# Block-sparse attention feeding a cosine router: x's writes on another queue, some copies and turns placed elsewhere

## The chip, the core and the metric

The kernel runs on one NeuronCore of one Trainium2 chip, in one launch. TensorE multiplies and transposes, VectorE (DVE), ScalarE (ACT) and GpSimd (POOL) work element by element, and transfers between DRAM and the on-chip memory are issued into queues by SyncE (SP), ScalarE or GpSimd and carried by 16 DMA engines. The metric is device time in microseconds, lower is better; a run gives one such time, and the median of several is quoted.

## The reference

Attention over 4 sequences, 8 heads, 768 positions and 64 numbers a head, in blocks of 32. A query block sees its neighbours, the first and the last block, and three blocks drawn for it; the first and last query block see all. The result goes, as 3072 rows x of 512 numbers, through a router that picks one of 8 experts by the cosine of x with an embedding, and through that expert:

```
scores = scale * q @ k.T;  scores = where(mask, scores, -1e9)
attn   = exp(scores - max) / (sum + 1e-9);   x = (attn @ v).transpose(0, 2, 1, 3).reshape(3072, 512)
logits = (x / |x|) @ (emb / |emb|).T / tau;  e = argmax(logits);  gate = softmax(logits)[e]
out    = gate * (relu(x @ w1[e]) @ w2[e])        # w1: 8 x 512 x 1024, w2: 8 x 1024 x 512
```

All of it is float32.

## The kernel before, in words

**Tiles.** A chunk is 128 queries of one sequence with all 8 heads; there are 24. Two chunks at the same place of two sequences are a duo (12 of them), and the loads, the routing and the rows of x go by duos. `pair_chunk` gives the place; place 0, which holds the first and last query block of a sequence, belongs to chunks 0, 1, 22 and 23, and these alone also do the "ends" (every key of the sequence).

**The attention loop** (`attention_fast`) has 25 steps s. In step s the scores of chunk `TURNS[s]` are made (`now`), the chunk of the step before is weighed with its values and normalized (`last`), the chunk of two steps before is transposed for the router (`past`, `turn_x`), and the next chunk's queries and keys are brought into shape (`after`). `TURNS` is 0, 2, 1, 3, 4, 5 and so on, so chunk 1 is scored in step 2. Nothing is reordered here: inside `manual_schedule` each engine and each queue does its work in the order of the code. Outside, in the expert tiles, a planner orders the instructions.

In one step TensorE does: `score_near` (L586, L589), `score_far` (L611), in even steps from 6 on `sum_logits` (L778), `turn_x` (L746), `turn_q` (L545), in steps 10 to 12 `turn_k` (L532), then weighs: `weigh_far`, the router's `part_logits` in odd steps (L768), `weigh_near` (all weighing is L666). ScalarE follows with the exponentials (L594, L616), the copies of own values `stack` in odd steps (L463), the copy of `part` (L770), the copy of the logits `take_logits` (L790) and the square of x (L736). VectorE has `gather_k` (L555), the copies after `turn_x` (L749) and `turn_q` (L550), the small operations of `route`, and `normalize` (L718, L720, L731). GpSimd copies the other gathered keys (L568) and values from neighbours (L511).

**Buffers that make work wait.** `turn_x` and `part_logits` share one PSUM buffer, `xg_ps`. The weighted sums `av` have one PSUM buffer, so `sum_logits` of a step, which opens it anew, waits until `normalize` of the step before has read it. The rows of x have three buffers, one per duo: `normalize` of duo s + 3 waits until duo s has been written to DRAM. The PSUM buffers "big" are two.

**Transfers.** In the loop every transfer but two query loads at the start is on SP's queue, in code order. Per step that is the gathering of 6 value blocks (`gather_v`, 128 KB each, address read from a register; L499), and between them loads of queries, keys and values (L497, L501). A gather for the next duo but one can be issued when `weigh_far` has read the buffer.

**The router** of a duo is a generator (`route`) whose six pieces `after_step` deals out over the steps that follow; the last piece writes x to DRAM (L887) and stands in the middle of a step (`planned(0)`): for duo 0 in step 7, for duo 1 in step 8, for duo b in step 2b + 6, up to duo 8 in step 22. Duo 0 has two pieces of rows, the others here one. Duos 9 and 10 are written behind the loop, when `k.attending` is false, and duo 11 during the first expert tile.

**The end of the loop.** Step 23 (chunk 22) and step 24 (chunk 23) are "ends" steps: `score_ends` for head pairs 0 and 2 (L642), `weigh_far`, `weigh_ends` for 0 and 2, `score_ends` for 1 and 3, `weigh_ends` for 1 and 3, `weigh_near`. The last step ends with the transposes of the first expert tile. Then 25 expert tiles follow, whose weights (2 MB each of w1 and w2) come on SP's queue.

The lines that the change touches most:

```
    copy = nc.scalar.copy if g % 2 or b == 0 else nc.vector.tensor_copy          # turn_k
    for half in range(1 if c == 0 else 0, 2):                                    # gather_k, near keys
        for z in range(2):
            lo = BLK * (NG * c + 2 * half - 2 + 3 * z)
            copy_by_one_port(k, t[:, :, 2 * half + z, lanes_of(NRAND, z)], kt[:, :, lo:lo + BLK])
    for rows, lo in pieces(c):                                                   # route, last piece
        nc.sync.dma_start(out=dram[lo:...], in_=x[rows]...)
```

Of the kernel before, what the change touches and what calls it, by code (L numbers as in the profile page):

```python
# [16 lines left out]
ALU = mybir.AluOpType  # L17
AX = mybir.AxisListType
# [3 lines left out]
B, H, S, D = 4, 8, 768, 64  # L22
BLK = 32
NB = S // BLK
NRAND = 3
NC = S // P
# [356 lines left out]
def lanes_of(slot, g):  # L383

    if slot < 2:
        return slice(BLK + slot, NRAND * BLK, 2)
    return slice(0, BLK) if (slot + g) % 2 == 0 else slice(NRAND * BLK, P)
# [126 lines left out]
def turn_k(k, g):  # L514

    nc = k.nc
    b, j = divmod(g, NPAIR)
    kt = k.kt[b % 2]
    raw = k.raw.pop(("k", g))
    copy = nc.scalar.copy if g % 2 or b == 0 else nc.vector.tensor_copy  # L520
    if b < DUO:
        ps = k.big.tile([P, 1024], F32, name="kps", tag="big")
        for r in range(NC):
            for h in range(2):
                lo = (h * NC + r) * D
                nc.tensor.matmul(ps[D * h:D * (h + 1), r * P:(r + 1) * P], lhsT=raw[:, lo:lo + D], rhs=k.ident,
                                 start=True, stop=True)
        copy(out=kt[:, j, 0:S].rearrange("p (t r) -> p t r", r=NC), in_=ps[:, 0:S].rearrange("p (r t) -> p t r", r=NC))  # L528
    else:
        ps = k.big.tile([P, 2, 512], F32, name="kps", tag="big")  # L530
        for c in range(NC):
            nc.tensor.transpose(ps[:, c // 3, c % 3 * P:(c % 3 + 1) * P], raw[:, c * P:(c + 1) * P], k.ident)  # L532
        copy(out=kt[:, j, 0:S].rearrange("p (w t) -> p w t", w=2), in_=ps[:, :, 0:3 * P])
    if j == NPAIR - 1:
        for i, block in enumerate((NB - 1, 0)):
            copy = nc.scalar.copy if i or b else nc.vector.tensor_copy
            copy(out=kt[:, :, S + i * BLK:S + (i + 1) * BLK], in_=kt[:, :, block * BLK:(block + 1) * BLK])  # L537
# [14 lines left out]

def copy_by_one_port(k, out, in_):

    k.nc.vector.tensor_reduce(out=out, in_=in_.unsqueeze(3), axis=AX.X, op=ALU.max)  # L555


def gather_k(k, n):

    nc = k.nc  # L560
    b, c, _ = place(n)
    kt = k.kt[b % 2]
    k.kg[n] = t = k.gp.tile([P, NPAIR, NG, P], F32, name="kg", tag="kg")
    for s in range(NRAND):
        engine, copy = ((mybir.EngineType.Pool, nc.gpsimd.tensor_copy) if s else
                        (mybir.EngineType.DVE, partial(copy_by_one_port, k)))
        for g, shift in zip(blocks_of(c), shifts(k, engine, s, c)):
            copy(out=t[:, :, g, lanes_of(s, g)], in_=kt[:, :, bass.ds(shift, BLK)])  # L568
    for half in range(1 if c == 0 else 0, 2):
        for z in range(2):  # L570
            lo = BLK * (NG * c + 2 * half - 2 + 3 * z)
            copy_by_one_port(k, t[:, :, 2 * half + z, lanes_of(NRAND, z)], kt[:, :, lo:lo + BLK])


def score_near(k, n):
# [72 lines left out]
def weigh_ends(k, n, pairs):  # L648

    _, c, i = place(n)  # L650
    for m in range(NC):
        for odd in range(2):
            for j in pairs:
                h = 2 * j + odd
                to = side(c, h, 0)
                weigh(k, n, slice(D * to, D * (to + 1)), h, k.pb[j][:, m, odd], k.vt[m][:, i, h])


def weigh(k, n, lanes, h, lhsT, rhs, last=False):

    av, begun = k.av[n]
    quads = [(h // NPAIR, q) for q in range(lanes.start // BLK, lanes.stop // BLK)]
    first = [q not in begun for q in quads]
    assert all(first) or not any(first)
    begun.update(quads)
    k.nc.tensor.matmul(av[lanes, h // NPAIR, h % NPAIR * P:h % NPAIR * P + D + 1], lhsT=lhsT, rhs=rhs, start=first[0],  # L666
                       stop=last, skip_group_check=True)
# [7 lines left out]
def weigh_near(k, n, turn):  # L675

    _, c, i = place(n)
    e, st = k.pac[n], k.st_ring[n // DUO % 2]
    for hh in range(2 * turn, 2 * turn + 2):
        for h in (hh, hh + NPAIR):  # L680
            for half in (1,) if c == 0 else (0, 1):
                to = side(c, h, half)
                weigh(k, n, slice(D * to, D * (to + 1)), h, e[:, h // 2, half, D * (h % 2):D * (h % 2 + 1)],
                      st[:, half, i, h], turn == 1)


def weigh_far(k, n, part):
# [147 lines left out]
def route(k, b):  # L835

    nc, p, x = k.nc, k.rp, k.x[b]
    many = NC if k.exact else DUO
    nrm = p.tile([P, many], F32, name="nrm") if k.exact else k.nsq[b]
    if k.exact:  # L840
        for c in range(NC):
            sq = p.tile([P, ND, P], F32, name="sq")
            nc.scalar.activation(sq, x[:, c, :, 0:P], ACT.Square, accum_out=nrm[:, c:c + 1])
    nc.gpsimd.tensor_tensor(out=nrm, in0=nrm, in1=k.half[:, 0:many], op=ALU.pow)

    def wide(t):
        return t.unsqueeze(2).broadcast_to([P, many, E])

    l = p.tile([P, many, E], F32, name="l")
    lg = logits(k, x) if k.exact else k.lg[b]  # L850
    yield
    nc.vector.tensor_scalar(out=nrm, in0=nrm, scalar1=1e-6, scalar2=None, op0=ALU.add)
    nc.vector.reciprocal(out=nrm, in_=nrm)
    m = p.tile([P, many], F32, name="mx")
    nc.vector.tensor_tensor(out=l, in0=lg, in1=wide(nrm), op=ALU.mult)
    nc.vector.reduce_max(out=m, in_=l, axis=AX.X)
    nc.vector.tensor_tensor(out=l, in0=l, in1=wide(m), op=ALU.subtract)
    yield
    ex = p.tile([P, many, E], F32, name="ex_l")
    nc.scalar.activation(ex, l, ACT.Exp)  # L860
    oh = k.oh[:, b * many:(b + 1) * many, :]
    pick = p.tile([P, many, E], F32, name="pick")
    nc.vector.tensor_scalar(out=pick, in0=l, scalar1=0.0, scalar2=None, op0=ALU.is_equal)
    nc.vector.tensor_tensor(out=pick, in0=pick, in1=k.rev.unsqueeze(1).broadcast_to([P, many, E]), op=ALU.mult)
    nc.vector.reduce_max(out=m, in_=pick, axis=AX.X)
    picked = nc.vector.tensor_tensor(out=oh, in0=pick, in1=wide(m), op=ALU.is_equal).ins
    yield
    for c in range(many):
        t = b * many + c
        nc.gpsimd.tensor_tensor(out=k.seen[:, t + 1, :], in0=k.seen[:, t, :], in1=k.oh[:, t, :], op=ALU.add)  # L870
    for w in (4, 2):
        nc.gpsimd.tensor_tensor(out=ex[:, :, 0:w], in0=ex[:, :, 0:w], in1=ex[:, :, w:2 * w], op=ALU.add)
    gate = p.tile([P, many, 1], F32, name="gate")
    nc.gpsimd.tensor_tensor(out=gate, in0=ex[:, :, 0:1], in1=ex[:, :, 1:2], op=ALU.add)
    nc.gpsimd.tensor_scalar(out=gate, in0=gate, scalar1=1e-9, scalar2=None, op0=ALU.add)
    yield
    with ExitStack() if k.attending else k.tc.issue_after(picked):
        nc.vector.reciprocal(out=x[:, :, :, P], in_=gate.broadcast_to([P, many, ND]))
    yield
    if k.exact:  # L880
        nc.sync.dma_start(out=k.x_dram[b * S:(b + 1) * S, :].rearrange("(c p) w -> p c w", p=P),
                          in_=x.rearrange("p c e w -> p c (e w)"))
        return
    a, c = pair_chunk(b)
    dram = k.x_dram[DUO * S * a:DUO * S * (a + 1), :].rearrange("(i s) w -> s i w", i=DUO)
    for rows, lo in pieces(c):
        nc.sync.dma_start(out=dram[lo:lo + rows.stop - rows.start], in_=x[rows].rearrange("p i e w -> p i (e w)"))  # L887


def rank(k, b):  # L890
# [424 lines left out]
def attention_fast(n, ctx):  # L1315
# [77 lines left out]
    for s in range(NCH + 1):  # L1393
# [25 lines left out]
        if not late_keys:  # L1419
            keys_gathered()  # L1420
        summed, n.parted = n.parted, None
        if summed is not None:
            sum_logits(n, last)
        if past is not None and past >= 2 * DUO:
            turn_x(n, past)
        elif past is not None and past % DUO:
            turn_x(n, past - 1)
        if ends:
            score_ends(n, last, 0)
            score_ends(n, last, 2)  # L1430
        elif after is not None and s:
            turn_q(n, after)
        if past is not None and past < 2 * DUO and past % DUO:
            turn_x(n, past)
        if not ends:
            turn_keys()
        planned(0)
# [53 lines left out]
        for m in values_at.get(s, ()):  # L1491
            loads += load_v(n, 1, m)
        fetch_all(n, gathers, loads)
        if ends:
            weigh_ends(n, last, (1, 3))
        if last is not None:
            weigh_near(n, last, 0)
            weigh_near(n, last, 1)
            normalize(n, last, summed)
        if s == 0:  # L1500
            build_consts(n)
            next(experts)
# [232 lines left out]
```

## Time and profile before

| | us |
|---|---|
| median of 3 runs | 613.65 (611.6 to 614.97) |
| the profiled execution | 615.24 |
| its span, first to last instruction | 613.5 |
| TensorE busy | 587.9 (96%) |
| GpSimd, VectorE, ScalarE busy | 243.5, 238.7, 146.2 |
| the chain that ended last: TensorE, VectorE, DMA, SP's queue | 73%, 7%, 7%, 6% |
| granted TensorE clock, mean | 0.993 |

The span has two parts. Up to 245.91 us, where the first expert matmul starts, the attention loop runs, with all engines at work; from there TensorE runs through the expert tiles with next to nothing between them. A busy share is an average over both. In the rows below, "L666" is a line of the code, `av<-vg,pd` is the tile written and the tiles read, and `[0.35 <-DVE xt L749]` says that the engine idled 0.35 us ahead of this instruction until VectorE's instruction of L749 was done. The loop's steps are cut at the first matmul of `score_near`: steps 4 to 9 start at 58.32, 67.08, 76.31, 83.51, 90.70 and 103.02 us, step 11 at 119.64, step 13 at 140.62, step 23 at 218.00.

### The profile page before, as it was taken

Reading aid. Unit: us, or ns where it says so; the run is one execution under the profiler, and the core shown is the slowest. Engines: PE = TensorE matmul, PEld = TensorE weight load, DVE = VectorE, ACT = ScalarE, POOL = GpSimd, SP = SyncE. Lnnn points to the kernel's source line nnn. Section 1 sums busy time; section 2 is a strip of 40 time slices with the busy share of each in tenths; the row PEclk is TensorE's granted clock in tenths of the full one; section 3 lists DMA queues with packets and bytes.
Section 4 is the critical chain, followed back from the end, with each engine's and each line's share of the span. In section 5 each row is a group of like instructions: output and inputs, shape, how many; then the busy total and the mean of one; then the engine's idle time right before and its main releaser. Section 6 shows DMA issues by size and latency. Waiting matters only on the chain.

```text
span 613.5 us, 18777 instructions
## 1 busy us (share of the span) xinstructions
PE 587.9 (96%) x7736; PEld 454.2 (74%) x7736; DVE 238.7 (39%) x744; ACT 146.2 (24%) x286; POOL 243.5 (40%) x474
## 2 busy tenths in 40 slices
PE   8999997989999988999999999999999999999995
PEld 5898797878898877777777777746777736777772
DVE  4463584667779942476211211112221121121110
ACT  3535663566555552100000000000000000000000
POOL 2637636447765430320333333333333333333332
PEclk9999998999999998999999999999999999999999
DMA  8989789789988731999999999998999998999511
GB/s 204 242 172 207 165 173 214 167 199 202 208 204 198 208 120 38 336 397 398 407 392 400 408 366 338 341 332 303 408 402 392 401 380 311 391 403 404 224 36 35
DMA packets 177073, 170.60 MB, mean 278 GB/s; under 512 B 135432, under 2 KB 137608, under 8 KB 174162
## 3 DMA queue, kind: packets, MB, share of 16 engines
q1 hardware_dynamic: 170706, 155.61, 78.8%
q0 software_dynamic: 5216, 13.43, 6.0%
q8 instruction: 63, 1.03, 0.7%
q10 hardware_dynamic: 1056, 0.26, 0.2%
q14 instruction: 32, 0.26, 0.1%
HBM read 156.65 MB, written 12.90 MB: 276 GB/s over the span
## 4 chain that ended last, share of the span: by engine, by line
PE 73%; DVE 7%; DMA 7%; SPq 6%; issue 3%; POOL 2%; ACT 1%; POOLq 0%; DVEq 0%; ACTq 0%
PE hp L1224 26%; PE yp L1237 25%; PE av L666 6%; SPq L499 4%; PE dps L611 4%; DMA vg<-in_v_dram 2%; PE hp L1269 2%; PE yp L1289 2%; DMA w<-in_moe_w_dram 2%; PE ac L586 2%; PE ac L589 2%; DVE qt L550 1%; PE bps L642 1%; PE xg_ps L746 1%; DVE xt L749 1%
## 5 line engine op out<-in xcount | busy, mean ns | idle before, releaser
L1224 PEld LDWEIGHTS hp<-xgt,w 128*128 128x128 f32 x1472 | 167.8, 192 | 10.9 <-issue 10.2
L1224 PE MATMUL hp<-xgt,w 128*128 128x128 f32 x1472 | 169.2, 276 | 0.3 <-DMA w<-in_moe_w_dram 0.3
L1237 PE MATMUL yp<-w,h 128*128 128x512 f32 x368 | 162.0, 593 | 0.0
L1237 PEld LDWEIGHTS yp<-w,h 128*128 128x128 f32 x368 | 68.2, 190 | 76.6 <-issue 76.2
L1148 POOL DMA_INDIRECT xg<-x_dram,quarter x88 | 89.2, 1014 | 32.3 <-issue 27.4
L1250 POOL DMA_INDIRECT out_dram<-y,slot_l x20 | 20.4, 1022 | 156.0 <-DVE y L1249 156.0
L1227 ACT ACTIVATE h<-hp 128x512 f32<-128x512 f32 x23 | 13.7, 597 | 283.2 <-PE hp L1224 280.2
L1231 DVE TENSOR_SCALAR h<-hp 128x512 f32<-128x512 f32 x23 | 15.9, 691 | 126.8 <-PE hp L1224 126.8
L568 POOL COPY kg<-kt 128x128 f32 x176 | 43.2, 294 | 30.2 <-ACT kt L528 21.0
L1249 DVE TENSOR_SCALAR y<-yp,gate 128x512 f32<-128x512 f32 x20 | 15.0, 751 | 102.2 <-PE yp L1237 90.1
L511 POOL COPY vg<-vt 32x1040 f32<-32x1040 f32 (+1 forms) x45 | 42.8, 951 | 18.9 <-PE av L666 13.0
L611 PEld LDWEIGHTS dps<-qt,kg 128*64 128x64 f32 x1408 | 46.9, 138 | 1.5 <-POOL kg L568 0.9
L611 PE MATMUL dps<-qt,kg 128*64 128x64 f32 x1408 | 46.6, 222 | 0.8 <-POOL kg L568 0.5
L586 PE MATMUL ac<-qt,kt 128*64 128x128 f32 x352 | 42.9, 274 | 0.5 <-DVE half L1378 0.5
L589 PE MATMUL ac<-qt,kt 128*64 128x256 f32 (+1 forms) x192 | 42.3, 364 | 0.3 <-ACT kt L537 0.3
L586 PEld LDWEIGHTS ac<-qt,kt 128*64 128x64 f32 x352 | 37.8, 137 | 0.9 <-issue 0.8
L550 DVE COPY qt<-yp 64x512 f32<-64x512 f32 x48 | 32.8, 684 | 12.0 <-PE yp L545 11.6
L616 ACT ACTIVATE pd<-dps,bias 128x256 f32<-128x256 f32 x88 | 34.7, 475 | 10.6 <-PE dps L611 10.6
L555 DVE TENSOR_REDUCE kg<-kt 128x128 f32<-128x128 f32 (+1 forms) x176 | 35.9, 275 | 3.0 <-ACT kt L528 1.2
L666 PE MATMUL av<-vg,pd 128*32 128x65 f32 x1408 | 30.4, 227 | 1.9 <-issue 0.8
L666 PEld LDWEIGHTS av<-vg,pd 128*32 128x32 f32 x1408 | 24.3, 113 | 7.7 <-issue 4.8
L666 PEld LDWEIGHTS av<-st,pac 128*64 128x64 f32 x704 | 23.5, 141 | 5.6 <-issue 4.8
(244 smaller groups left out, 599.3 us busy)
## 6 DMA issues: line engine op xcount, KB each, us to landing
w<-in_moe_w_dram SPq DMA_DIRECT2D x52, 2048.0 KB, 15.3
vg<-in_v_dram SPq DMA_DIRECT2D x132, 128.0 KB, 4.0
kraw<-in_k_dram SPq DMA_DIRECT2D x32, 192.0 KB, 4.5
x_dram<-x SPq DMA_DIRECT2D x10, 516.0 KB, 4.5
qraw<-in_q_dram SPq DMA_DIRECT2D x9, 512.0 KB, 4.9
w<-in_moe_w_dram SPq DMA_DIRECT2D x8, 512.0 KB, 5.8
vt<-in_v_dram SPq DMA_DIRECT2D x10, 256.0 KB, 4.5
vt<-in_v_dram SPq DMA_DIRECT2D x5, 512.0 KB, 7.4
```

The source lines that it names most:

```text
L511: k.nc.gpsimd.tensor_copy(out=k.vg_ring[s % 2][lanes_of(NRAND, g), g, which(i)], in_=k.vt[m][rows, which(i)])
L550: k.nc.vector.tensor_copy(out=t[rows, :, h], in_=ps[rows])
L555: k.nc.vector.tensor_reduce(out=out, in_=in_.unsqueeze(3), axis=AX.X, op=ALU.max)
L568: copy(out=t[:, :, g, lanes_of(s, g)], in_=kt[:, :, bass.ds(shift, BLK)])
L586: nc.tensor.matmul(out[0:D, j, half], lhsT=kt[:, j, at:at + D], rhs=qt[:, j, :, D * half:D * (half + 1)], start=True, stop=True)
L589: nc.tensor.matmul(out[D:P, j, half:2].rearrange("p f h t -> p h f t"), lhsT=kt[:, j, S:S + D], rhs=qt[:, j, :, D * half:P].rearrange("p h ...
L611: nc.tensor.matmul(out[D * r:D * (r + 1), NG * j + g], lhsT=kg[:, j, g, D * r:D * (r + 1)], rhs=qt[:, j, :, cols], start=True, stop=True)
L616: nc.scalar.activation(e[:, :, g].rearrange("p j h t -> p j (h t)"), out.rearrange("p (j g) h t -> p j g (h t)", g=NG)[:, :, g], ACT.Exp, ...
L666: k.nc.tensor.matmul(av[lanes, h // NPAIR, h % NPAIR * P:h % NPAIR * P + D + 1], lhsT=lhsT, rhs=rhs, start=first[0], stop=last, skip_group ...
L1148: k.nc.gpsimd.indirect_dma_start(out=x[:, g], out_offset=None, in_=quarters, in_offset=bass.IndirectOffsetOnAxis(ap=k.quarter[:, g, t:t + ...
L1224: nc.tensor.matmul(hp[:, f, :], lhsT=w1[:, d, (f0 + f) * P:(f0 + f + 1) * P], rhs=xt[:, d, :], start=(d == 0), stop=(d == ND - 1))
L1237: nc.tensor.matmul(yp, lhsT=h[:, f, :], rhs=w2[:, f, :], start=(f == 0), stop=(f == NF - 1))
```

## The change

Six edits, none of which changes what is computed:

- the last piece of `route` issues the write of x on ScalarE's queue instead of SP's while the attention loop runs;
- the four copies of neighbouring keys per chunk in `gather_k` become two, each over two blocks (in chunks at place 0 there were two, and there are two);
- K pair 10, turned in step 11, is copied out of PSUM by ScalarE instead of VectorE;
- `turn_x` of chunk 0 moves from step 4 to step 2, that of chunk 2 from step 5 to the end of step 4, those of chunks 1 and 3 stay in their steps;
- in the last step `score_ends` for pairs 0 and 2 comes ahead of `sum_logits` and `turn_x`;
- in the four "ends" steps `weigh_ends` for pairs 1 and 3 comes behind `weigh_near`. The `stop` flag of the matmuls follows the new last one.

```
@@ turn_k
-    copy = nc.scalar.copy if g % 2 or b == 0 else nc.vector.tensor_copy
+    copy = nc.scalar.copy if g % 2 or b == 0 or g == 3 * NPAIR - 2 else nc.vector.tensor_copy
@@ copy_by_one_port
-    k.nc.vector.tensor_reduce(out=out, in_=in_.unsqueeze(3), axis=AX.X, op=ALU.max)
+    k.nc.vector.tensor_reduce(out=out, in_=in_.unsqueeze(len(in_.shape)), axis=AX.X, op=ALU.max)
@@ gather_k
-    for half in range(1 if c == 0 else 0, 2):
-        for z in range(2):
-            lo = BLK * (NG * c + 2 * half - 2 + 3 * z)
-            copy_by_one_port(k, t[:, :, 2 * half + z, lanes_of(NRAND, z)], kt[:, :, lo:lo + BLK])
+    halves = 1 if c == 0 else 2
+    for z in range(2):
+        lo = BLK * (NG * c + 2 * (2 - halves) - 2 + 3 * z)
+        copy_by_one_port(k, t[:, :, 4 - 2 * halves + z::2, lanes_of(NRAND, z)],
+                         kt[:, :, lo:lo + BLK].unsqueeze(2) if halves == 1 else
+                         kt[:, :, lo:lo + 2 * D].rearrange("p j (f t) -> p j f t", f=2)[:, :, :, 0:BLK])
@@ weigh_ends, weigh_near (the stop flags)
+                      m == NC - 1 and 3 in pairs)
-                      st[:, half, i, h], turn == 1)
+                      st[:, half, i, h], turn == 1 and c != 0)
@@ route
+    queue = nc.scalar if k.attending else nc.sync
     for rows, lo in pieces(c):
-        nc.sync.dma_start(out=dram[lo:lo + rows.stop - rows.start], in_=x[rows].rearrange("p i e w -> p i (e w)"))
+        queue.dma_start(out=dram[lo:lo + rows.stop - rows.start], in_=x[rows].rearrange("p i e w -> p i (e w)"))
@@ attention_fast, one step
+        if s == NCH:
+            score_ends(n, last, 0)
+            score_ends(n, last, 2)
         if summed is not None:
             sum_logits(n, last)
-        if past is not None and past >= 2 * DUO:
+        if past is not None and past != 2:
             turn_x(n, past)
-        elif past is not None and past % DUO:
-            turn_x(n, past - 1)
-        if ends:
+        if ends and s < NCH:
             score_ends(n, last, 0)
             score_ends(n, last, 2)
         elif after is not None and s:
             turn_q(n, after)
-        if past is not None and past < 2 * DUO and past % DUO:
-            turn_x(n, past)
...
-        if ends:
-            weigh_ends(n, last, (1, 3))
         if last is not None:
             weigh_near(n, last, 0)
             weigh_near(n, last, 1)
+            if ends:
+                weigh_ends(n, last, (1, 3))
             normalize(n, last, summed)
+        if past == 1:
+            turn_x(n, 2)
```

## Rows read from the trace of the kernel before

**Rows 1.** The page's first part: busy time, share of the span, instructions.

```profile
PE 587.9 (96%) x7736; PEld 454.2 (74%) x7736; DVE 238.7 (39%) x744; ACT 146.2 (24%) x286; POOL 243.5 (40%) x474
```

**Rows 2.** The waits: waiter, what it waited for, us, times, longest.

```profile
DVE x L731 <- DMA x_dram<-x: 5.7, 1, 5.7
```

**Rows 3.** Stretches: us, busy by engine, TensorE clock, DMA share, GB/s.

```profile
58.32:76.31 17.99, 16.60 (x420) 14.50 (x417) 11.21 (x32) 11.31 (x20) 9.59 (x23) 1.00 0.74 164
76.31:83.51 7.20, 7.20 (x202) 6.87 (x200) 5.66 (x21) 3.59 (x9) 0.00 (x0) 1.00 0.82 182
90.70:103.02 12.32, 8.77 (x202) 8.31 (x200) 4.88 (x17) 3.78 (x9) 7.24 (x19) 0.86 0.93 191
99.40:103.00 3.60, 3.60 (x98) 3.36 (x98) 1.97 (x4) 1.81 (x5) 1.39 (x2) 0.53 1.18 196
...
119.64:130.94 11.30, 9.84 (x224) 8.66 (x222) 7.86 (x26) 7.18 (x15) 3.24 (x10) 1.00 0.85 199
140.62:149.09 8.47, 8.05 (x207) 6.94 (x205) 7.49 (x26) 5.95 (x12) 5.42 (x17) 1.00 0.98 206
...
236.00:246.00 10.00, 9.34 (x337) 8.71 (x337) 1.02 (x2) 3.13 (x4) 0.67 (x1) 0.83 0.12 45
```

**Rows 4.** Issues of DMAs: by line (ns min/median/max), and one of SP.

```profile
L887 SPq DMA_DIRECT2D x_dram<-x x14: 372/505/5666, 91.5 to 272.2; - x14
L1340 ACTq DMA_DIRECT2D qraw<-in_q_dram x2: 417/444/472, 0.8 to 1.3; - x2
L499 SPq DMA_DIRECT2D vg<-in_v_dram x132: 317/597/4186, 11.6 to 208.2; - x132
93.29 3.59 SPq L499 DMA_DIRECT2D vg<-in_v_dram  x1
```

**Rows 5.** The chain that ended last, two pieces: start, us, what.

```profile
92.17 4.94 DMA x_dram<-x
...
142.44 3.78 DMA vg<-in_v_dram
```

**Rows 6.** TensorE in order of time, steps 7 and 8.

```profile
88.24 1.11 PE L666 MATMUL av<-vg,pd 128*32 128x65 f32 x64
89.72 1.15 PE L666 MATMUL av<-st,pac 128*64 128x65 f32 x32
...
98.03 0.58 PE L778 MATMUL av<-sel,part 128*128 128x8 f32 x4 [3.55 <-DVE x L878]
...
99.47 1.96 PE L666 MATMUL av<-vg,pd 128*32 128x65 f32 x64
101.36 1.83 PE L666 MATMUL av<-st,pac 128*64 128x65 f32 x32
```

**Rows 7.** ScalarE in order of time, steps 7 and 14.

```profile
87.34 1.57 ACT L616 ACTIVATE pd<-dps,bias 128x256 f32<-128x256 f32 x4 [0.40 <-PE dps L611]
...
156.51 0.17 ACT L790 COPY lg<-av 128x16 f32<-128x16 f32 x1 [2.02 <-PE av L666]
```

**Rows 8.** TensorE in order of time, steps 2 and 4.

```profile
42.16 1.10 PE L666 MATMUL av<-vg,pd 128*32 128x65 f32 x58 [0.20 <-DMA vg<-in_v_dram]
...
63.51 0.66 PE L746 MATMUL xg_ps<-ident,x 128*128 128x128 f32 x4 [0.35 <-DVE xt L749]
```

**Rows 9.** TensorE in order of time, step 11.

```profile
127.68 0.88 PE L532 MATMUL kps<-ident,kraw 128*128 128x128 f32 x6 [1.12 <-DVE kt L533]
```

**Rows 10.** Groups of instructions by line and shape, 0 to 245 us.

```profile
L555 DVE TENSOR_REDUCE kg<-kt 128x128 f32 x88 | 19.0, 276 | 3.0 <-ACT kt L528 1.2 <-DVE kt L537 0.7 <-ACT kt L533 0.7
```

**Rows 11.** TensorE in order of time, step 24.

```profile
234.64 0.58 PE L778 MATMUL av<-sel,part 128*128 128x8 f32 x4 [1.35 <-DVE x L731]
...
235.92 2.84 PE L642 MATMUL bps<-qt,kt 64*64 64x64 f32 x96
...
241.28 1.63 PE L642 MATMUL bps<-qt,kt 64*64 64x64 f32 x96
...
243.89 1.55 PE L666 MATMUL av<-vt,pb 128*64 128x65 f32 x45 [0.37 <-ACT pb L644]
```

More of the change, by code (lines that the diff above doesn't have):

```diff
@@ L655, in weigh_ends @@
                 to = side(c, h, 0)
-                weigh(k, n, slice(D * to, D * (to + 1)), h, k.pb[j][:, m, odd], k.vt[m][:, i, h])
+                weigh(k, n, slice(D * to, D * (to + 1)), h, k.pb[j][:, m, odd], k.vt[m][:, i, h],
+                      m == NC - 1 and 3 in pairs)
 def weigh(k, n, lanes, h, lhsT, rhs, last=False):
```

## Prediction

> **What bounds the kernel now.** The first view is the page's busy line [rows 1]: TensorE is busy 587.9 of 613.5 us. The rest, 25.6 us, and the matmuls that ran at half clock are all that this change can win, for it takes no arithmetic out. Second come the waits [rows 2]: one stands alone, 5.7 us of VectorE at `normalize` (L731) for a transfer of x to DRAM. Third come stretches cut at the first score matmul of each step s of the attention loop [rows 3]. Step 6 shows what a step costs when nothing is late: 7.20 us, TensorE busy for all of it. Steps 4 and 5 take 17.99 together, step 8 takes 12.32, step 11 takes 11.30, step 13 takes 8.47. The same rows show the second limit: the DMA engines' share is 0.93 in step 8, 1.18 in its last 3.6 us, and 0.98 in step 13. So TensorE sets the end, and the transfers stand close behind. After the attention loop the expert tiles run back to back, so time won before them moves the end.
>
> **x's writes on ScalarE's queue.** Ten writes move, those of duos 0 to 8; duo 0 has two pieces. On SP one takes 0.505 us in the median, on ScalarE the only two transfers of the trace took 0.444 [rows 4]. So SP loses 10 x 0.505 = 5.05 us of issuing and ScalarE gains 4.4. The first one matters most. `normalize` of step 7 writes duo 3 into the buffer of duo 0, and duo 0's second piece, issued on SP at 92.17 behind the gathers, needed 4.94 us to land, until 97.11 [rows 5]; this is L731's wait [rows 2], and the next `sum_logits` on TensorE started after 3.55 of waiting [rows 6]. On ScalarE the write stands behind `score_far`'s exponentials of step 7, which end at 87.34 + 1.57 = 88.91 [rows 7]. Two issues put the second piece at 89.4; with the same 4.94 it lands at 94.3, which is 2.8 earlier. I take 2.8 off the 3.55 of idle time; 0.75 stays. After the 3.55 the granted clock was 0.53 for 3.6 us [rows 3], the 1.2 GHz level for nearly all of it: weighing took 1.96 + 1.83 where step 7's took 1.11 + 1.15 [rows 6]. An idle time of 0.75 is shorter than the 1.12 of step 11 [rows 9], after which that step shows clock 1.00 [rows 3]; so the 1.53 goes too. Step 8: **4.3**. Bounds: 1.5 if the clock still falls and the piece lands 1.3 later; 5.1 if nothing is left.
>
> What waits behind a write on ScalarE: in even steps the copy of the logits, `take_logits`, before which ScalarE stands idle for 2.02 us (step 14 [rows 7]). Nine moved writes therefore cost nothing on the path while an issue stays under 2 us. In step 7 the two pieces push the stack copies and the copy of `part` by 0.9; `part` is needed by `sum_logits` nearly 4 us into step 8, so that is covered too.
>
> **x turned elsewhere.** Before, steps 4 and 5 each transpose two chunks through the one buffer `xg_ps`, with VectorE's copy between, which is behind the query copies: four waits like the 0.35 at 63.51 [rows 8], 17.99 - 16.60 = 1.39 us of idle TensorE over both steps [rows 3]. After, chunk 0 is turned in step 2, where TensorE waits for gathered values anyway (its weighing goes on at 42.16, released by a gather [rows 8]), chunk 2 at the end of step 4. One group of transposes (0.66, of which some 0.5 is not overlapped by the next) leaves the two steps as well. **1.9**; bounds 0.5 (a new wait of `xg_ps` for the copy of `part` at the end of step 4) and 2.4.
>
> **The K copy on ScalarE (step 11).** TensorE waits 1.12 us for VectorE's copy of pair 10 before it can turn pair 12 [rows 9]; VectorE was at query copies. ScalarE has done its exponentials of the step by then, so its copy can start with the end of pair 10's matmuls. **1.1**; bounds 0 (ScalarE then queues two copies before pair 12) and 1.3.
>
> **Merged neighbouring keys.** 20 chunks go from four VectorE reductions of 128x128 to two of 128x256. The group's mean is 276 ns [rows 10]; merging saves at most two of them per chunk, 11 us of VectorE in all, and below nothing if the wider form costs over twice as much. VectorE is busy for 5.66 of step 6's 7.20 us [rows 3] and has room, so I take 0 on the path, bounds -1 and +1.
>
> **The order at the ends.** In step 24 TensorE idles 1.35 before `sum_logits`, which needs L731 to have read `av`; then the 96 matmuls of `score_ends` take 2.84, while the same 96 take 1.63 later [rows 11] (the clock of 236 to 246 is 0.83 [rows 3]). After, these 96 run first and fill VectorE's time: 1.35 + 1.21 = 2.56. A new wait takes some back: `weigh_ends(0, 2)` then needs exponentials that stand on ScalarE behind the square of chunk 22; I take 0.4. Then `weigh_near` between the last `score_ends` and `weigh_ends(1, 3)`: its 16 matmuls, about half of the 1.15 that 32 take [rows 6], fill the 0.37 of waiting shown [rows 11] and the like before it; 0.6 in each of steps 23 and 24 and 0.4 in step 3. In step 1 it is worth nothing, because step 2 waits for gathered values. **3.4** at the end, bounds 1.0 and 4.5, and **0.4** in step 3.
>
> **What is late next.** The terms before step 13 are 0.4 + 1.9 + 4.3 + 1.1 = 7.7 us. But in step 13 TensorE already waits for values whose last gather was issued at 142.44 and landed 3.78 later, at 146.22 [rows 5]; the step is 8.47 long instead of 7.20. SP's stream of issues is what these values wait for: a gather takes 0.597 us to issue in the median, the one behind duo 0's write 3.59, the longest 4.19 [rows 4]. TensorE would now want the values 7.7 earlier. SP is ahead by the four writes that no longer stand in front, 4 x 0.505 = 2.0; if the two long issues shrink to 0.6 as well, by another 6.6. So between 5.7 us and nothing of the 7.7 is given back. I take 3.5, nearer the large end, since the engines' share stands at 0.93 and above in steps 8 and 13, where these bytes must pass. Behind step 13 the six later writes leave SP, and waits of steps 13 to 19 (1.27 in step 13 and smaller ones) ease: +1.0.
>
> The sum is 7.7 - 3.5 + 1.0 + 3.4 = **8.6**. I take 8, because the farther end of what is given back is the larger one. The profiled execution took 615.24 (span 613.5 and 1.7 around it): 607.2. That execution lies 1.6 above the median of the runs, 613.65, against which the same gain gives 605.7. I say **606.5**.
>
> On x's writes the Trainium skill ("DMA: Bandwidth & Descriptors", section "Issuing engines are not separate DMA queues") speaks against the change: transfers from all queues share the same 16 engines, and a second issuer saves only the time to issue. By that, the sum would go as in rival A. The shares of steps 8 and 13 [rows 3] agree with it for these steps; x on a second queue the trace does not show.
>
> **Rivals.**
> A. The transfers are the bound: the bytes of x still pass the same engines, only from another queue, the gathers land no earlier, and whatever TensorE wins up to step 12 is waited for in step 13. For it: the shares of 0.93 and 0.98 in steps 8 and 13. Against it: 0.74 in steps 4 and 5 and 0.85 in step 11 [rows 3], so there is room. What is left is the end (3.4) and 0.5: 615.24 - 3.9 = 611.3, some 610 against the median.
> B. SP's full queue was the bound: with x gone from it the gathers keep ahead. Nothing is given back, and steps 13 to 19 lose 2: 7.7 + 2 + 3.4 = 13.1, 602.1. For it: the 3.59 right behind the write of x, six times the median. Against it: a load of queries stands between the two, so plain bytes can cause it as well.
> C. Slower: ScalarE is held at the issue. Its stream is in order, so a write that takes as long as the longest gather issue, 4.19, delays `take_logits`, `normalize` and the next `sum_logits` by 4.19 - 2.02 = 2.2 us in each of nine steps: 20 more, 627. It decides from 2 us per issue. For it: the longest write on SP took 5.67. Against it: the median is 0.505 [rows 4], and ScalarE's own queue holds nothing else.
> D. The write lands no earlier (it shares the engines with the gathers and loads queued at 88 to 92) and the clock falls as before: step 8 keeps its length. Of the other 3.4 before step 13 half stays, and 3.4 at the end: 615.24 - 5.1 = 610.1.
>
> **How the numbers follow.** Forecast (gain 5.5 to 10.5) 0.50, A 0.20, B 0.16, C 0.07, D 0.07. Below 0.5%, 3 us, this kernel's runs (611.6 to 614.97) cannot tell a change from none. Forecast and B are faster; A and D, at gains of 3.9 and 5.1 with as much doubt below as above, lie near the edge: half of them count as faster, the other half as the same. Faster 0.50 + 0.16 + 0.13 = 0.79, same 0.14, slower 0.07. The range goes from B's time to just over A's and D's: 601.5 to 612.5. The forecast's own is 603 to 609.
>
> **What would show it.** The wait of L731 for x falls from 5.7 to near 3, and step 8 is 8 us long at clock 1.00. The writes at L887 stand on ScalarE's queue at 0.4 to 0.6 us each. No wait for `xt` in steps 4 and 5, none for L533 in step 11. Steps 23 and 24 lose over 3 us and keep clock 1.00 behind 236. Gathers: the wait in front of L666 of step 13 is longer than 1.3, or step 9 shows a new one. It is wrong if the attention loop shrinks by under 5 or over 11 us, if the expert tiles change length, or if an issue on ScalarE takes over 2 us.

## The result, and the profile after

The changed kernel takes 622.43 us (median of 4 runs, 620.47 to 623.17), the kernel before 614.01 beside it: ratio 1.0142, 95% interval 1.0113 to 1.0171. It is slower by 8.4 us; 606.5 was forecast. The profiled execution took 622.51, its span is 620.7.

Busy line of the page after, for [rows 1]:

```profile
PE 589.4 (95%) x7736; PEld 454.5 (73%) x7736; DVE 234.7 (38%) x703; ACT 147.4 (24%) x287; POOL 244.1 (39%) x474
```

TensorE does the same work in 1.5 us more (587.9 before) and stands idle 5.7 us longer. Where it does so, the table by steps says, cut like [rows 3] at the first score matmul (length, busy time of each engine, granted TensorE clock, DMA engines' share, GB/s): steps 4, 5, 7, 8, 9, 11, 13.

```profile
58.46:66.77 8.31, 7.95 (x211) 6.99 (x207) 5.97 (x17) 5.56 (x10) 2.88 (x4) 1.00 0.78 174
66.77:74.45 7.68, 7.68 (x205) 7.03 (x206) 4.27 (x11) 5.54 (x10) 7.13 (x20) 1.00 0.81 160
81.65:98.39 16.74, 10.17 (x207) 8.58 (x205) 6.98 (x25) 5.95 (x12) 11.16 (x33) 0.80 0.55 131
98.39:105.64 7.25, 7.25 (x202) 6.92 (x200) 4.53 (x13) 3.32 (x7) 0.84 (x1) 1.00 0.91 227
105.64:118.79 13.15, 9.81 (x209) 8.11 (x205) 6.24 (x22) 5.96 (x12) 8.06 (x26) 0.87 0.94 153
127.35:139.53 12.18, 10.48 (x225) 8.87 (x223) 7.49 (x25) 8.08 (x16) 4.56 (x17) 1.00 0.55 128
149.20:157.99 8.79, 8.04 (x206) 6.93 (x204) 7.38 (x23) 5.96 (x12) 5.74 (x18) 1.00 0.88 205
```

Steps 4 and 5 (15.99 together, 17.99 before) came out as forecast, and step 8 (7.25, 12.32 before) a little shorter than the forecast 8. Step 7 went from 7.19 to 16.74, step 9 from 8.06 to 13.15. In step 7 the DMA share is only 0.55: the transfers are not crowded, they are missing. TensorE's rows in step 7 show what it waits for:

```profile
86.38 0.30 PE L669 MATMUL av<-vg,pd 128*32 128x65 f32 x2
90.67 0.30 PE L669 MATMUL av<-vg,pd 128*32 128x65 f32 x2 [3.98 <-DMA vg<-in_v_dram]
92.92 0.40 PE L669 MATMUL av<-vg,pd 128*32 128x65 f32 x2 [1.95 <-DMA vg<-in_v_dram]
93.95 1.83 PE L669 MATMUL av<-vg,pd 128*32 128x65 f32 x57 [0.64 <-DMA vg<-in_v_dram]
```

Gathered values (vg) are late by 6.57 us in all, and then the 57 matmuls take 1.83 at the 1.2 GHz level (granted clock 0.50; in e1 below 57 take 1.01 at 1.00). From the view of waits, all of the run (us, times, longest): what TensorE waited for before and after, and below it what SP's queue waited for after:

```profile
PE av L666 <- DMA vg<-in_v_dram: 0.6, 3, 0.2
```

```profile
PE av L669 <- DMA vg<-in_v_dram: 14.8, 17, 4.0
```

```profile
SPq L499 <- DMA x_dram<-x: 29.3, 7, 7.9
...
SPq L497 <- DMA x_dram<-x: 1.2, 1, 1.2
```

What SP waits for is the key. SP, which in the loop no longer writes x, waits 30.5 us for writes of x before it issues *gathers of V* and one load of keys, which move other data into other buffers; before, it waited for none. [Rows 2]' wait of L731 for x is gone. SP's queue, ScalarE's queue, and the chain of waits around step 7 (start, duration):

```profile
78.66 0.37 SPq L497 DMA_DIRECT2D kraw<-in_k_dram  x1
79.22 8.73 SPq L499 DMA_DIRECT2D vg<-in_v_dram  x2
89.15 0.40 SPq L497 DMA_DIRECT2D kraw<-in_k_dram  x1
```

```profile
85.55 0.32 ACTq L891 DMA_DIRECT2D x_dram<-x  x1
...
85.91 0.45 ACTq L891 DMA_DIRECT2D x_dram<-x  x1
```

```profile
85.91 3.22 DMA x_dram<-x
89.15 0.40 SPq L497
...
89.74 0.40 SPq L499
...
90.36 3.55 DMA vg<-in_v_dram
...
93.95 1.83 PE av L669 x57
```

Of the two gathers under 79.22 the second is issued at 87.61; between them SP does nothing. The write of duo 0 stands on ScalarE behind the exponentials of step 7 and is issued only at 85.55, just after the first of them has started (85.48). When its two pieces land SP goes on, at 87.61 and 89.15, and TensorE goes on when the gathers behind that have landed. Step 9 repeats it with duo 1, whose write ScalarE issues at 102.28: SP stands still for 5.2 us until 107.12.

The compiled program says why. Every transfer of SP and ScalarE counts its landing on one of eight counters (DMAHW0 to 7), dealt out in turn over both queues, and before it is issued the transfer that had its counter last must have landed. From its list of instructions (number, line, tile written and tile read, shape, the counters waited for), first ScalarE, then SP:

```
69 L891 DMA x_dram_60<-x_816 32x2x516 [waits DMAHW5_49,DVE_49]
70 L891 DMA x_dram_60<-x_816 96x2x516 [waits DMAHW6_49]

129 L499 DMA vg1_115<-in_v_dram 32x16x64 [waits DMAHW7_49]
130 L497 DMA qraw_1597<-in_q_dram 128x16x64 [waits DMAHW0_49]
...
138 L499 DMA vg1_115<-in_v_dram 32x16x64 [waits DMAHW4_49]
140 L499 DMA vg1_115<-in_v_dram 32x16x64 [waits DMAHW5_49]
141 L497 DMA kraw_1600<-in_k_dram 128x6x64 [waits DMAHW6_49]
```

The two pieces of x have counters 5 and 6, a turn ahead of SP's row 129. SP may issue six more; rows 140 and 141 must wait for x. In the kernel before the write stood on SP itself, 18 transfers later, when x was there; all turns were then taken in the order of issue.

### The profile page after: what moved, and what is told of

Its sections match the earlier page's. It is cut to its first block, busy times and chain, and to the rows that moved or that the text cites. A ratio compares the mean times of both kernels' runs of the same rounds, so it can differ in the third digit from the quotient of the medians.

```text
span 620.7 us, 18737 instructions
## 1 busy us (share of the span) xinstructions
PE 589.4 (95%) x7736; PEld 454.5 (73%) x7736; DVE 234.7 (38%) x703; ACT 147.4 (24%) x287; POOL 244.1 (39%) x474
## 4 chain that ended last, share of the span: by engine, by line
PE 75%; DMA 10%; SPq 6%; DVE 3%; issue 2%; ACT 1%; POOL 1%; POOLq 0%; DVEq 0%; ACTq 0%
PE hp L1228 27%; PE yp L1241 25%; PE av L669 6%; DMA x_dram<-x 5%; SPq L499 5%; DMA vg<-in_v_dram 4%; PE dps L613 3%; PE hp L1273 2%; PE yp L1293 2%; PE ac L588 1%; DMA kraw<-in_k_dram 1%; PE bps L644 1%; PE ac L591 1%; PE kps L526 1%; PE xg_ps L771 1%
## 5 line engine op out<-in xcount | busy, mean ns | idle before, releaser
L1152 POOL DMA_INDIRECT xg<-x_dram,quarter x88 | 89.4, 1016 | 32.3 <-issue 27.4
L669 PE MATMUL av<-vg,pd 128*32 128x65 f32 x1408 | 32.5, 226 | 15.4 <-DMA vg<-in_v_dram 14.8
L669 PEld LDWEIGHTS av<-vg,pd 128*32 128x32 f32 x1408 | 25.0, 112 | 22.6 <-DMA vg<-in_v_dram 15.6
L618 ACT ACTIVATE pd<-dps,bias 128x256 f32<-128x256 f32 x88 | 34.7, 475 | 11.5 <-PE dps L613 11.4
L555 DVE TENSOR_REDUCE kg<-kt 128x128 f32 (+2 forms) x136 | 33.5, 315 | 3.0 <-ACT kt L528 1.2
```

The lines of the kernel that those rows point to most:

```text
L555: k.nc.vector.tensor_reduce(out=out, in_=in_.unsqueeze(len(in_.shape)), axis=AX.X, op=ALU.max)
L618: nc.scalar.activation(e[:, :, g].rearrange("p j h t -> p j (h t)"), out.rearrange("p (j g) h t -> p j g (h t)", g=NG)[:, :, g], ACT.Exp, ...
L1152: k.nc.gpsimd.indirect_dma_start(out=x[:, g], out_offset=None, in_=quarters, in_offset=bass.IndirectOffsetOnAxis(ap=k.quarter[:, g, t:t + ...
```

## The experiments

The theory to test ("counters"): x's write holds counters that SP's gathers need. Rival 1 ("bytes"): x's bytes push the gathers aside on the 16 DMA engines. Rival 2: the other edits are to blame. Ratios are to the kernel before on the same chip.

**All writes back on SP** (`e1_x_on_sp`)

```diff
-    queue = nc.scalar if k.attending else nc.sync
+    queue = nc.sync
```

> The changed kernel with x's writes put back on SyncE's queue; all other edits stay. Theory (counters): in the compiled program the transfers of SP and of ScalarE take turns at eight completion counters, and a transfer is issued only when the eighth before it has landed; so SP's gathers stand and wait until x's write, which ScalarE issues late, is done (SPq L499 <- DMA x_dram<-x: 29.3 us in the changed kernel, none before). Without it that wait is 0, steps 7 and 9 are 7.5 and 8 us again instead of 16.7 and 13.2, and VectorE's 5.7 us wait for x in step 8 comes back: the four other edits keep about 2.0 (steps 4, 5), 1.1 (step 11) and 3.7 (end) less 2 to 4 given back, 607 to 611 us. Rival 1 (x's bytes push the gathers aside on the 16 engines): the same 607 to 611. Rival 2 (the moved transposes and the other order hold the gathers up, not the queue): 618 or more.

Measured 609.93, ratio 0.9949 (0.9916 to 0.9982). SP has no wait for x; steps 7, 8 and 9 last 7.66, 11.65 and 8.47. Rival 2 is out: the other edits are a gain. Rival 1 expected the same time here, so this run says nothing on it.

**The queue alone** (`e2_only_queue`), the kernel before with

```diff
-        nc.sync.dma_start(out=dram[lo:...
+        (nc.scalar if k.attending else nc.sync).dma_start(out=dram[lo:...
```

> The kernel before with x's writes on ScalarE's queue and nothing else changed. Theory (counters): SP's gathers wait for x by 25 to 35 us in all, steps 7, 9 and 11 grow as in the changed kernel; against the kernel before +10 to +14 us, 624 to 628. Rival 1 (bytes): the same sign, +5 to +14. Rival 2 (the other edits are to blame): the queue alone is a gain, 608 to 611.

Measured 626.22, ratio 1.0255 (1.0188 to 1.0322). SP waits 33.2 us for x; steps 7, 8 and 9 last 15.40, 7.20 and 13.02. The queue alone costs 15.6 us, and the other edits give some back.

**Other counters: GpSimd's queue** (`e5_x_on_pool`), `queue = nc.gpsimd if k.attending else nc.sync`.

> The changed kernel with x's writes of the attention loop issued by GpSimd instead of ScalarE: the same bytes at nearly the same moments on the same 16 engines, but counted on other counters than SP's. Theory (counters): SP has no wait for x, steps 7, 8 and 9 are each 7.2 to 9 us, 602 to 608 us in all. Rival 1 (bytes): steps 7 and 9 stay at 13 us or more, 617 to 623. What neither theory prices: GpSimd's own time for issuing, which no row here shows; over 2 us each it would show in its gather copies (kg).

Measured 611.79, 0.9998 (0.9972 to 1.0024). SP waits for no write; steps 7 and 9 are 7.44 and 7.98 long, so there the counters theory holds and that of the bytes doesn't. The time lies outside my 602 to 608 because of step 8, which lasts 15.33: GpSimd issued duo 0's write only at 91.2, and VectorE waited 8.5 us for it.

**A later turn** (`e4_place10`, then `i1_place6`): all of x on ScalarE as in the change, but each write made to wait for a certain earlier transfer of SP, so that its turn comes behind it.

```diff
+        if k.attending:   # put = the write; fetched = SP's loads and gathers in the order of the code
+            k.tc.add_manual_dep(put.ins, k.fetched[-10].name, mybir.DependencyInfo(   # [-6] in i1
+                mybir.DependencyClass.Sync, mybir.DependencyReason.DATA), ...)
```

> The changed kernel, x's writes on ScalarE's queue, each made to wait for the transfer of SP that is tenth from the end of those programmed ahead of it; its only purpose is that x's write takes its turn at the counters later, behind that transfer, so that SP may run about seven transfers further before it meets x's counter. Theory (counters): SP's waits for x fall from 29.3 us to under 12, step 7 from 16.7 to 7.5 to 10, in all 605 to 613 us. Rival 1 (bytes): the same bytes pass at the same time or later, 617 to 623, step 7 stays over 13.

> The changed kernel, all of x's writes of the loop on ScalarE's queue, each made to take its turn at the counters behind the sixth last transfer of SP ahead of it, where the run before had the tenth last. A third dose beside the changed kernel itself (SP waits 30.5 us for x, steps 7 and 9 at 16.7 and 13.2) and the tenth place (17.1 us). Theory (counters): SP's waits for x fall again, to under 10 us; step 7 is 7.2 to 8.5 and the time 608 to 614. If the wait that ScalarE now has for that transfer holds its own stream up, steps 7 to 9 stay over 28 us together and the time is 613 to 618.

With the tenth, SP waits 17.1 us for x and steps 7 to 9 take 30.98 (37.14 in the changed kernel); the time is 616.59, ratio 1.0077 (1.0049 to 1.0106). That is less of each, though I expected under 12 us of waiting and 605 to 613. Step 7 is back at 7.19, but step 9 takes 16.59. With the sixth, the waits of SP on x come down to

```profile
SPq L499 <- DMA x_dram<-x: 4.1, 5, 1.9
```

and steps 7, 8 and 9 to

```profile
81.57:88.76 7.19, 7.19 (x206) 6.54 (x204) 6.77 (x24) 3.59 (x9) 5.25 (x16) 1.00 0.97 198
88.76:97.70 8.94, 7.25 (x203) 6.88 (x201) 4.65 (x15) 5.59 (x10) 6.62 (x18) 1.00 0.91 212
97.70:110.59 12.89, 9.60 (x208) 8.12 (x204) 6.13 (x22) 5.95 (x12) 8.15 (x26) 0.87 0.90 188
```

The time is 609.25, ratio 0.9921 (0.9893 to 0.9949). Bytes and queue are the same; what changed is the turn, and ScalarE's wait for it, by which duo 0's write goes out later (86.93 instead of 85.55). From 30.5 over 17.1 to 4.1 us of waiting the ratio goes 1.0142, 1.0077, 0.9921. Step 9 is still 12.89; more on that below.

**Nearly no bytes** (`h1_one_row`): x on SP, and in the place of each write on ScalarE one row there.

```diff
+        if k.attending:
+            nc.scalar.dma_start(out=k.spare[...], in_=x[rows.start:rows.start + 1, 0].rearrange("p e w -> p (e w)"))
```

> The changed kernel with all of x's writes on SP, and in the place of each of the ten writes that the change put on ScalarE a write there of one row of x (2 KB) to a part of DRAM that nothing reads. Nearly no bytes, but each takes its turn at the counters as x's write did in the changed kernel. Theory (counters): SP's gathers wait for these rows as they waited for x, 20 to 32 us in all; step 7 lasts 13 to 17 us, and the time is 616 to 624 us. Rival 1 (bytes): 2 KB cost nothing, 608 to 612 us as with x on SP alone.

SP's queue, its waits before gathers (2.0 us before a load come on top), and the windows 76 to 80, 80 to 84, 84 to 88:

```profile
78.60 0.38 SPq L497 DMA_DIRECT2D kraw<-in_k_dram  x1
79.16 8.57 SPq L499 DMA_DIRECT2D vg<-in_v_dram  x2
87.85 0.42 SPq L497 DMA_DIRECT2D kraw<-in_k_dram  x1
```

```profile
SPq L499 <- DMA spare<-x: 12.7, 4, 7.7
```

```profile
76.00:80.00 4.00, 4.00 (x89) 3.93 (x86) 2.91 (x13) 2.85 (x7) 0.00 (x0) 1.00 0.98 221
80.00:84.00 4.00, 4.00 (x123) 3.74 (x123) 3.72 (x12) 0.82 (x5) 0.96 (x5) 1.00 0.35 78
84.00:88.00 4.00, 3.30 (x77) 2.90 (x73) 3.90 (x13) 3.57 (x9) 3.73 (x10) 1.00 0.01 3
```

A row of 2 KB stops SP at the same gather for 7.7 us, where the 129 KB piece of x did for 7.2 (and the 387 KB piece for 1.2 more at the load behind it), while the DMA engines run dry (3 GB/s). With x on SP alone, no such row, the last two windows show

```profile
80.00:84.00 4.00, 4.00 (x127) 3.91 (x118) 3.62 (x14) 0.94 (x4) 1.53 (x7) 1.00 0.90 197
84.00:88.00 4.00, 3.79 (x126) 3.23 (x121) 3.99 (x11) 3.60 (x8) 3.71 (x10) 1.00 0.78 170
```

The time is 615.06, ratio 1.0049 (1.0026 to 1.0072); step 7 lasts 14.69. That is 1.0% above e1, about half of what the changed kernel lost. SP's 14.7 us of waiting and the time lie under my 20 to 32 and 616 to 624. A likely reason, not tested by itself: a row lands sooner (issued at 86.17, SP goes on at 87.39) than a full write (6.2 us in the median), so that later duos hold SP less. That ten rows of 2 KB cost 6 us, and step 7 grows by 7.0 against e1, can't be due to bytes.

**Twice the bytes** (`g2_twice`): e1, and each write once more on GpSimd's queue into a spare part of DRAM.

> The changed kernel with x's writes on SP, and every one of the attention loop's ten writes made once more by GpSimd's queue to a part of DRAM that nothing reads: twice the bytes of x, none of them on a counter that SP waits for (the second copy also holds x's buffer longer). Theory (counters): bytes cost little, 609 to 614 us, SP waits for no write of x, steps 7 and 9 stay under 9. Rival 1 (bytes): the second copy costs what the changed kernel lost against this one, 12 us or more: 618 to 626.

The time is 619.41, ratio 1.0094 (1.0059 to 1.0128): the number is the rival's, not mine. The trace takes it apart. From the start of step 9 to that of step 22 this run needs 111.3 us, e1 109.5 and its repetition (j2 below) 107.9, so the second copies cost 1.8 to 3.4 us over thirteen steps, GpSimd's time to issue them included; steps 7 and 9 are 7.19 and 7.99. The loss is step 8 (18.03), where VectorE waits for x's buffer, held by the late second copy (waits from 85 to 115 us):

```profile
DVE x L734 <- DMA spare<-x: 11.1, 1, 11.1
```

**Duo 0 alone on ScalarE**: as in the change (`g1_duo0`), with the tenth place (`f2_duo0_place`), and that with duos 1 to 8 on GpSimd (`f1_duo0_place_pool`).

```diff
+    queue = nc.scalar if k.attending and b == 0 else nc.sync                        # g1, f2
+    queue = nc.sync if not k.attending else nc.gpsimd if b else nc.scalar           # f1
```

> The changed kernel with only duo 0's write of x left on ScalarE's queue; the eight later ones are back on SP. Theory (counters): one stall of SP's gathers is left, the one that ends with duo 0's write near 87.6 us. Step 7 lasts 14 to 17 us, step 8 7.3, step 9 and the odd steps behind it are as with all writes on SP (8.5, 9.7) or shorter, since the gathers get ahead while TensorE stands. Against the kernel with all writes on SP (609.9): +9 in step 7, -4.4 in step 8, 0 to -4 in step 13: 610 to 615 us. Rival 1 (bytes): one write of 516 KB passes as it did from SP, step 7 stays under 9 and the time is 605 to 608.

> The changed kernel with duo 0's write on ScalarE's queue and made to take its turn at the counters behind the tenth last transfer of SP ahead of it, as in the run with that place for all writes; the later writes are on SP. Theory (counters): steps 7 and 8 are both 7.2 to 8 us, as there, and no later write stops the gathers; against all writes on SP (609.9) -4.4 in step 8 and +1 to +3 given back in steps 9 to 13: 606 to 609 us. If step 8 only passes its wait on to step 9, 609 to 611.

> As the run before it, but the writes of duos 1 to 8 issued by GpSimd, on counters of its own. Theory (counters): steps 7 and 8 at 7.2 to 8 us as in the run with the later place, steps 9 and 13 at 8.0 and 7.5 to 9 as in the run with all writes on GpSimd, whose only large loss was step 8 (15.3, a late write of duo 0): 602 to 607 us. If a write of GpSimd's queue is late in the later duos too, VectorE waits for x there and it is 607 to 612.

g1 has ratio 1.0001 (0.9972 to 1.0031), with step 7 at 16.29 and step 8 at 7.84: one write, one stall, some 3 us more than e1. f2 has 0.9945 (0.9917 to 0.9974), no better than e1, and f1 0.9983 (0.9949 to 1.0017), outside my 602 to 607 us. Both have step 8 at 7.20, and step 9 at 14.08 and 16.96. What step 8 won is waited for in step 9, mostly for gathers; SP still lost 2.9 (f2) and 3.1 us (f1) to x there.

**The other edits one by one**: the ends' order on the kernel before (`h2_ends`), the transposes and the K copy on it (`h4_turn`), and e1 with the near keys copied apart (`h3_apart`); each is its hunk of the diff.

> The kernel before with only the new order at the ends (score_ends first in the last step, weigh_near between the two parts of the ends). The prediction priced it at 3.4 us in steps 23 and 24 (1.0 to 4.5) and 0.4 in step 3: 0.994 to 0.996 of the time before. Rival: ScalarE's exponentials and VectorE's reads are late next, steps 23 and 24 keep 27 us, 0.999 to 1.000.

> The kernel before with only the moved transposes and the K copy on ScalarE. The prediction priced them at 1.9 (steps 4 and 5) and 1.1 (step 11). If the gathers give nothing back: 0.995 of the time before. If TensorE only reaches its wait for gathers in steps 8 to 13 earlier, what it won is waited for there: 0.998 to 1.001. With the later steps' gathers as late as before I expect the second, about 0.999.

> The changed kernel with x's writes on SP and the copies of neighbouring keys not merged, as in the kernel before. The prediction priced the merging at 0 on the path (-1 to +1 us): as the run with all writes on SP, 0.993 to 0.997 of the time before. VectorE's group L555 should be back at 176 reductions of some 276 ns. Rival: VectorE's 10 us set the steps in which TensorE waits for VectorE, then 0.998 or more.

The ratios are 0.9983 (0.9964 to 1.0002), 0.9987 (0.9966 to 1.0007) and 0.9963 (0.9943 to 0.9984). The first lies between my 0.994 to 0.996 and the rival's 0.999 to 1.000; the second is what I expected if the gain is waited for later. The third is e1 within the interval: merging is worth nothing on the path. VectorE's group L555 of the changed kernel,

```profile
L555 DVE TENSOR_REDUCE kg<-kt 128x128 f32 (+2 forms) x136 | 33.5, 315 | 3.0 <-ACT kt L528 1.2 <-DVE kt L537 0.7 <-ACT kt L533 0.7
```

is 40 instructions fewer and 2.4 us less busy than without the merge (h3: 176 of 276 ns, 35.9 us in all; [rows 10] shows one form of it).

**The kernel before, twice more** (`b2_before`, `b3_before`), no edit.

> The kernel before, unchanged, profiled once more. Its first profiled execution lay 1.6 us above the median of its runs, and the prediction took the ends' term (3.4) from that one. If the idle 1.67, 0.65, 1.35 and the clock of 0.83 in steps 23 and 24 belong to every execution, these steps last 27 to 28 us again; if they are one execution's, 24 to 26, and the term was mis-sized by the difference.

> The kernel before, unchanged, profiled a third time, for the same question: steps 23 and 24 at 27 to 28 us if the term belongs to every execution, at 24 to 26 if not.

They took 616.72 and 612.4 us. Steps 23 and 24, up to the first expert matmul, last 25.3 and 23.8 us, against 27.9 in the first profile: by the bounds set ahead, that profile was a long one, and the term read from it can be too large. Some of it belongs to the kernel all the same. In all six profiles with the old order these steps last 23.8 to 27.9, mean 25.9; in the fourteen with the new order 21.8 to 24.6, mean 23.0. From step 22's first score matmul to the end of the span the means are 400.6 (398.6 to 403.3) and 397.4 (395.1 to 399.9).

**The two mended versions side by side, and the mended queue alone** (`j1_place6` and `j2_x_on_sp` are i1 and e1 again; `j3_queue_place6` is e2 with the sixth place).

> The changed kernel with the sixth place once more, beside the kernel with x's writes on SP on the same chip, to tell which of the two is the better version. If a write on ScalarE that holds no gather up is worth more than the 2 us it frees on SP: 0.990 to 0.993 of the time before, clear of the other; if the gathers behind it are the limit anyway, 0.993 to 0.996 for both.

> The changed kernel with x's writes on SP once more: 0.992 to 0.997 of the time before.

> The kernel before with x's writes on ScalarE's queue, in the sixth place, and nothing else changed: the counterpart of the run with the queue alone, which took 1.0255. Theory (counters): with the place moved the loss goes, 0.995 to 1.003. Rival (the queue itself, by bytes or by ScalarE's time): 1.015 or more.

The ratios are 0.9909 (0.9873 to 0.9944), 0.9892 (0.9851 to 0.9933), and 1.0050 (1.0019 to 1.0080). Over all four measurements the mended versions beat the kernel before by 3 to 7 us, and they can't be told apart. The later turn takes 12.6 of the queue's 15.6 us away (1.0255 to 1.0050); 3 us stay, more than my 0.995 to 1.003 allowed. SP still waits 6.4 us for x in that run; whether this is all of it I did not settle.

## Why the prediction was wrong

**The step that failed** is the one on SP's stream: "SP is ahead by the four writes that no longer stand in front", from which the gathers could only come earlier, or, in rival A, at the same time. I priced what SP issues and not what it waits for before it issues: 30.5 us of waiting for x, where I had put none. With all transfers on one queue a turn at the counters is taken when SP gets there, so a late x held nothing that was not behind it anyway. On a second queue the turn is dealt out early and the write issued late. The trace of before had a sign, in the list of SP's waits:

```profile
SPq L501 <- DMA qraw<-in_q_dram: 2.0, 1, 2.0
```

This is a load of keys at 5.63 us, which waits for one of the two query loads that ScalarE issues at the start [rows 4], data that it does not use. A transfer that waits for an unrelated one shares something with it.

The Trainium skill ("DMA: Bandwidth & Descriptors", section "Anatomy of one DMA — SWDGE (gpsimd) path") says that DMA engines never wait on semaphores; the wait is made by the sequencer that issues. The trace agrees: in h1 SP stands 7.7 us at one gather while the engines' share falls to 0.35 and then 0.01. The rule of the Trainium skill that the prediction weighed, that a second issuer saves only the time to issue, led to rival A's gain of 3.9 us; none of my rivals, the slower C included, had this loss in it.

**Step 8's 4.3** was right where it was put and worth nothing in the time. The write went out at 85.55, earlier than my 89.4: step 7 began 1.86 us earlier, and the issue did not wait for the exponentials to end. L731's wait vanished, and step 8 took 7.25. (In i1 and j1, where the write goes out later, 4.0 and 3.5 us of that wait are back, and step 8 takes 8.94 and 8.39.) But f2, f1, i1 and j1, in which SP loses little to the counters, keep steps 7 to 9 at 28.8 to 31.4 us together, against 27.6, 29.9 and 27.4 in three profiles of before and 27.8 and 28.7 in e1 and j2. I had let 3.5 be given back behind step 12 over all terms; here step 9 alone takes the whole 4.3, gathers being late (2.92 at 105.65 in i1) and the clock of 0.87 following the idle time. In i1 this is not the counters: SP waits for no x between 80 and 110 us there. From the chain of waits there, the gather that TensorE waits for in step 9 (start; us from issue to landing, where the median gather of the kernel before takes 4.0):

```profile
99.62 6.67 DMA vg<-in_v_dram
```

The DMA share of that step is 0.90. This points to rival A's mechanism, full transfers, for what is left once the counters are mended; no run tests it alone. In j3 steps 7 to 9 do get shorter, 25.8 together, but step 22 starts at 214.29 (212.24 before): the gain is lost again on the way.

**ScalarE's side** held: an issue takes 0.37 us there (median of ten), rival C's 2 us are far off. **The transposes**: 1.9 forecast, 17.99 to 15.99. **The K copy**: TensorE's wait for VectorE in front of L532 is gone; step 11 goes from 11.30 to 9.70 in e1 and 11.04 in j2 (1.1 forecast), where TensorE stands 1.21 elsewhere in the step, for a reason that the profile doesn't show; in the changed kernel it is 12.18, from late gathers. Timed together without the other edits (h4), the transposes and the K copy are worth 0.8 us (loss of 0.4 to gain of 2.1) of the 3.0 forecast. **Merged keys**: 0 forecast, none found. **The ends**: 3.4 forecast, from a profile that was long there; some 3 us by the means of the twenty profiles (2.9 in steps 23 and 24); timed alone, 1.0 us (loss of 0.1 to gain of 2.2). These two don't agree, and I leave that open. All of these together: 6.8 less what is given back was the forecast; timed, 3.1 (e1) and 6.6 us (j2).

So 8.4 us slower is 3.1 to 6.6 gained by the other edits and 11.5 to 15 lost on the queue, most of it at the counters: with the queue alone, 12.6 of 15.6 us go when only the turn is moved.

## What to carry to other kernels

Before a transfer moves to another queue, look in the compiled program at which completion counter it takes, after which transfers of the other queue, and when its own engine will reach it: a late issue with an early turn stops the queue that it was meant to relieve. In a profile the sign is a queue that waits for a transfer whose data it does not touch, with the DMA share low. And a wait removed in front of a stream that is itself just in time is found again one step later: price the next gather before the wait.

## What was not expected of the hardware

A 2 KB write held SP's queue at the same gather as long as a 129 KB one did (7.7 and 7.2 us), and the DMA engines fell to 3 GB/s meanwhile. Twice the bytes of x cost 1.8 to 3.4 us over thirteen steps. GpSimd took 0.78 us to issue a write of x, where ScalarE took 0.37 and SP 0.505 [rows 4].
